# Moving small steps within a fused attention and expert kernel: where sums are finished, how token slots are made, when the hash codes come back, and how the first pair is laid out

## The chip, the cores and the metric

The kernel runs on one core of one Trainium2 chip. The metric is device time in microseconds (us). Engines are named as in the profile: PE multiplies matrices, PEld loads its weights, DVE, ACT and POOL work on vectors, and SP issues nearly all transfers from one queue, in order ("SPq"). L12 is line 12 of the kernel before.

## The reference

What is computed, cut to what matters here:

```python
q_bits = (einsum('bhsd,dk->bhsk', q, proj) > 0)      # 6 bits, k_bits alike
mask = q_bucket[:, :, :, None] == k_bucket[:, :, None, :]
scores = where(mask, q @ k.T / sqrt(D), -1e9)        # B 4, H 8, S 768, D 64
attn = exp(scores - max); attn /= attn.sum(-1) + 1e-09
x = (attn @ v) laid out as 3072 tokens of 512
probs = softmax(x @ w_gate)                          # 8 experts, the best one is taken
out[token] = gate * (relu(x[token] @ w1[e]) @ w2[e]) # w1 512 x 1024, w2 1024 x 512
```

## The kernel before

The attention works on 16 pairs of heads (`NPAIR` 4 per batch, `NPR` 16 in all). A pair has two groups of three blocks of 128 rows for two heads: twelve steps `(pr, g, jj, hh)`, 192 in all. The loop over `steps` is written with one step as its unit, and PE, DVE, ACT and SP run their instructions in just the order of the program; POOL's instructions are placed by a scheduler, apart from those wrapped in `in_turn`, which keep the program's order among themselves. Here `n` is the step in the group, and (g, n) names a place in a pair.

In step i the program issues the scores of step i + 2 (`scores`, L229 and L230 on PE, then the row maximum L232 and one or two small operations L233, L236 on DVE), the exponent of step i + 1 (`expo`, L248 on ACT, which also adds up the row into `sums`), the turning of the probabilities of step i or i - 1 (on PE and ACT, L273 and L276, or for half of the blocks through DRAM: four transfers `moved<-pd` L258, one back `pq<-moved` L261 two steps later, and a DVE transposition L264 six steps after the block), and in odd steps the product with V of the group before (`av`, L291). PSUM has two tiles for scores, so scores of step i + 2 wait for the exponent of step i.

Beside this stand slower threads:

- **Sums.** In step 5 of a group `av_evac` copies the product of the group before and adds 1e-9 to its sums: on POOL (L306, `in_turn`) in nearly all groups. Two steps later, `out_and_route` takes the reciprocal on DVE (L307), and `av_out` multiplies by it (L324).
- **Next pair's operands.** `PREPARE` lists at which place `q_operands`, `k_operands` (three POOL operations each, L160 to L162 and L169 to L171) and `pair_codes` (PE L146, DVE L148, POOL L149) are issued. The codes go to DRAM (`codes_out`, L175) and come back reshaped as rows of the second operand (`codes_back`, two transfers `c<-coded`, L180), which the scores L230 read.
- **Routing.** When a batch's four pairs are done, `route` makes pieces which run one to a step from the list `light`: `logits`, `gather_heads`, `one_hot`, `pause`, `ranks`, `rows`. Group 0's `rows` falls at (1, 3) of the second pair after, group 1's at (0, 4) of the next. In `rows` DVE makes the slots (L388 to L391) and POOL writes the rows to DRAM with three indirect transfers (L393). `gather_heads` and `av_out` use the same single PSUM tile `misc`, which `one_hot` reads last (L371).
- **The start.** `first_k` and `first_q` build the first pair's operands; `CLEARS` says in which steps the eight 910 KB fills of `xs` are issued.

After step 191 and a last routing, the experts follow: eight times two layers of matmuls on PE, with each operand split in two parts.

## Time and profile before

| | us |
|---|---|
| median of 3 runs | 755.05 |
| lowest and highest | 750.77 and 755.68 |
| the profiled execution's own time | 751.78 |
| its span, first to last instruction | 749.6 |
| first row maximum of step 0 / of step 12 / of step 192's last | 9.23 / 40.13 / 455.65 |

The span stretches from the first instruction to the last; the profiled execution's own time lies 2.2 us above it. A timeline row gives start, duration, engine, line, operation, tiles and, in brackets, how long its engine stood idle before it and what ended that. A row of a stretch (windows) gives its length, the busy time of each engine, the share of the full TensorE clock granted, and what the transfers took.

### The profile page before, as it was taken

The numbers are of one execution on the slowest core, as the hardware profiler recorded it, in microseconds if no ns is written. First come the engines' busy times: TensorE is split into PE (matmuls) and PEld (weight loads), VectorE is DVE, ScalarE is ACT, GpSimd is POOL, SyncE is SP. The second block draws the span as 40 slices with busy tenths as digits, with TensorE's granted clock in tenths as the row PEclk, the third lists the DMA queues.
The fourth block names the chain that finished last, engine by engine and source line by source line (L and its number), as shares of the span: only waits on it lengthen the run. The fifth ranks groups of instructions, "written<-read, shape, count | busy, mean of one in ns | idle before, by whom it ended". The sixth has DMA issues, their size and how long they took to land.

```text
span 749.6 us, 16080 instructions
## 1 busy us (share of the span) xinstructions
PE 706.7 (94%) x5735; PEld 621.4 (83%) x5735; DVE 520.1 (69%) x1028; ACT 465.3 (62%) x995; POOL 411.9 (55%) x401
## 2 busy tenths in 40 slices
PE   5999999988999979999979898999999999999996
PEld 2788887777887768887768787999999999999994
DVE  6668887867888867888868676674646464675741
ACT  5788987867988767898766674352434343443430
POOL 2775657485657575565675252105555647475471
PEclk9999999999999998999989999999999999999999
DMA  8969888877888877887885621646475565757521
GB/s 276 298 175 266 249 238 265 273 216 236 261 237 251 281 237 200 273 256 216 259 269 153 164 85 45 169 133 193 128 191 138 176 167 178 198 172 209 172 76 45
DMA packets 110081, 150.33 MB, mean 201 GB/s; under 512 B 12548, under 2 KB 77990, under 8 KB 109992
## 3 DMA queue, kind: packets, MB, share of 16 engines
q1 hardware_dynamic: 105016, 136.52, 63.6%
q0 software_dynamic: 4976, 12.69, 4.8%
q8 instruction: 47, 0.77, 0.4%
q14 instruction: 42, 0.34, 0.2%
HBM read 94.23 MB, written 55.18 MB: 199 GB/s over the span
## 4 chain that ended last, share of the span: by engine, by line
issue 20%; POOL 14%; PE 10%; DVE 4%; DMA 4%; SPq 1%; POOLq 0%; ACT 0%; another core or an unknown queue 0%; DVEq 0%
POOL y L1010 11%; PE o L291 3%; PE t L273 2%; PE s L229 2%; POOL yo L1008 2%; DMA y<-yo,tok 1%; PE s L230 1%; DVE m L232 1%; DMA xr<-xs 1%; DMA c<-coded 1%; PE s L722 1%; POOL tags L931 0%; DMA moved<-pd 0%; DVE pt L264 0%
## 5 line engine op out<-in xcount | busy, mean ns | idle before, releaser
L232 DVE TENSOR_REDUCE m<-s 128x1 f32<-128x768 f32 x192 | 182.8, 952 | 68.3 <-PE s L230 52.1
L229 PE MATMUL s<-k,q 128*128 128x512 f32 (+1 forms) x384 | 152.0, 396 | 19.7 <-ACT pd L248 11.8
L291 PE MATMUL o<-pt,vt 128*64 128x128 f32 x2304 | 148.6, 279 | 0.0
L291 PEld LDWEIGHTS o<-pt,vt 128*64 128x64 f32 x2304 | 125.6, 138 | 17.3 <-issue 11.5
L230 PE MATMUL s<-c 76*128 76x512 f32 (+1 forms) x384 | 127.0, 351 | 3.5 <-DMA c<-coded 3.4
L276 ACT COPY pt<-t 128x384 f32<-128x384 f32 x222 | 96.2, 485 | 54.3 <-PE t L273 51.5
L1010 POOL DMA_INDIRECT y<-yo,tags x88 | 104.1, 1183 | 24.9 <-issue 22.6
L229 PEld LDWEIGHTS s<-k,q 128*128 128x128 f32 x384 | 75.0, 195 | 51.3 <-POOL k L169 11.7
L248 ACT ACTIVATE p<-s,m 128x768 f32<-128x768 f32 x111 | 110.3, 994 | 10.7 <-DVE m L236 7.2
L273 PE MATMUL t<-ident,p 128*128 128x128 f32 x666 | 95.7, 281 | 0.0
L968 ACT ACTIVATE hh<-hps 128x352 fp32r<-128x352 f32 (+3 forms) x56 | 27.9, 500 | 97.5 <-PE hps L982 82.1
L230 PEld LDWEIGHTS s<-c 76*128 76x128 f32 x384 | 75.7, 197 | 14.2 <-issue 4.5
L273 PEld LDWEIGHTS t<-ident,p 128*128 128x128 f32 x666 | 77.9, 144 | 10.9 <-issue 9.8
L691 DVE TENSOR_TENSOR wlo<-wraw,whi 128x1024 fp32r<-128x1024 f32 x60 | 73.3, 1224 | 18.3 <-ACT whi L686 16.6
L248 ACT ACTIVATE pd<-s,m 128x768 f32<-128x768 f32 x81 | 80.3, 992 | 4.6 <-DVE m L236 0.7
L264 DVE STREAM_TRANSPOSE pt<-pq 128x768 f32<-128x768 f32 x81 | 78.5, 969 | 2.8 <-DMA pq<-moved 2.7
L1001 PE MATMUL hps<-hh,whi 128*128 128x448 f32 (+9 forms) x224 | 75.7, 338 | 0.0
L1001 PE MATMUL hps<-hl,whi 128*128 128x436 f32 (+6 forms) x224 | 75.6, 338 | 0.0
L1001 PE MATMUL hps<-hh,wlo 128*128 128x436 f32 (+6 forms) x224 | 75.6, 338 | 0.0
L982 PE MATMUL hps<-xh,whi 128*128 128x352 f32 (+3 forms) x224 | 75.2, 336 | 0.0
L982 PE MATMUL hps<-xl,whi 128*128 128x428 f32 (+6 forms) x224 | 74.9, 335 | 0.0
L982 PE MATMUL hps<-xh,wlo 128*128 128x428 f32 (+6 forms) x224 | 74.7, 334 | 0.0
(222 smaller groups left out, 1192.9 us busy)
## 6 DMA issues: line engine op xcount, KB each, us to landing
wraw<-w SPq DMA_DIRECT2D x64, 512.0 KB
moved<-pd SPq DMA_DIRECT2D x324, 96.0 KB
pq<-moved SPq DMA_DIRECT2D x81, 384.0 KB
qk<-qkd SPq DMA_DIRECT2D x30, 384.0 KB
xs<-zrow SPq DMA_DIRECT2D x8, 910.0 KB
vt<-v SPq DMA_DIRECT2D x16, 384.0 KB
coded<-cr SPq DMA_DIRECT2D x15, 192.0 KB
c<-coded SPq DMA_DIRECT2D x30, 72.0 KB
```

The costliest lines, as they stand in the source:

```text
L229: PE.matmul(out=s[:, c0:c1], lhsT=q1[:, qs], rhs=k1[:, c0:c1], start=True, stop=False)
L230: PE.matmul(out=s[:, c0:c1], lhsT=q2[0:KM, qs], rhs=k2[0:KM, c0:c1], start=False, stop=True)
L232: V.tensor_reduce(out=m[:, 0:1], in_=s[:, 0:S], axis=AX.X, op=ALU.max, negate=True)
L248: A.activation(to, of, AF.Exp, bias=m[:, 2:3], scale=m[:, 1:2], accum_out=sums[:, idx:idx + 1])
L264: V.transpose(out=pt()[:, hh].rearrange("p c (s j) -> p c s j", j=SQ), in_=q.rearrange("p s c i -> p c s i"))
L273: PE.transpose(out=t[:, i * P:i * P + P], in_=p[:, kc * P:kc * P + P], identity=ident)
L276: A.copy(out=dst, in_=src)
L291: PE.matmul(out=o[hh * D:hh * D + D, jj * P:jj * P + P], lhsT=vt[:, kc, hh * D:hh * D + D], rhs=pt[:, hh, kc], start=kc == 0, stop=kc == N ...
L691: loeng.tensor_tensor(out=lo[:, i:i + step], in0=cell["t"], in1=bf(hi[:, i:i + step]), op=ALU.subtract)
L982: PE.matmul(out=hps[:, 0:w], lhsT=wt[:, c, fs], rhs=xt[:, c, 0:w], start=n == 0, stop=n == 3 * NDC - 1)
L1001: PE.matmul(out=yps[:, 0:w], lhsT=wt[:, f, ds], rhs=ht[:, 0:w], start=n == 0, stop=n == 3 * NFC - 1)
L1010: rows_apart("out", G.indirect_dma_start(out=out_seg, out_offset=bass.IndirectOffsetOnAxis(ap=tags[:, i, 0:1].bitcast(I32), axis=0), in_=y ...
```

## The change

It has six parts. (1) The addition of 1e-9 to a group's sums is issued in step 0 of the next group, on POOL, in all groups but the last, and no longer in step 5. (2) `rows` takes the slot as a row maximum that is written as an integer (there is one non-zero entry) in place of a sum, and adds 1e-9 through a tensor operand `tiny` in place of a constant; the cast is gone, and the first of its three POOL transfers is held in the program's order. (3) Group 1's routing too has a `pause` behind `one_hot`, and group 0's `rows` issues the next piece, `av_out`, in the same step. (4) `codes_back` stands in step (1, 0) ahead of the returning `pq` transfer and the loads, and for the last pair in step (0, 5) of the pair before. (5) In the first pair `pair_codes` goes ahead of the second half of `first_q`, which is issued one step later; the scaling of the second head's codes comes behind the second exponent; two constant copies on DVE move to step 4; the next pair's operands and codes are prepared earlier. (6) `CLEARS` is earlier by a step or two.

```diff
-        if defer:
-            in_turn(G.tensor_scalar(out=sums, in0=sums, scalar1=1e-9, scalar2=None, op0=ALU.add))
             divide.append(lambda: V.reciprocal(out=inv, in_=sums.rearrange("p (j h) -> p j h", h=2)))
         else:
-            V.tensor_scalar(out=sums, in0=sums, scalar1=1e-9, scalar2=None, op0=ALU.add)
...
+        if n == 0 and prev is not None:
+            in_turn(G.tensor_scalar(out=prev[2], in0=prev[2], scalar1=1e-9, scalar2=None, op0=ALU.add))
...
         def rows():
-            V.tensor_scalar(out=mx[:, :, 1:2], in0=mx[:, :, 1:2], scalar1=1e-9, scalar2=None, op0=ALU.add)
-            V.reduce_sum(out=mx[:, :, 3:4], in_=pos, axis=AX.X)
+            V.reduce_max(out=slot, in_=pos, axis=AX.X)
+            V.tensor_tensor(out=mx[:, :, 1:2], in0=mx[:, :, 1:2], in1=tiny.unsqueeze(1).broadcast_to([P, 3, 1]), op=ALU.add)
             V.reciprocal(out=x[:, :, :, SEG + 1], in_=mx[:, :, 1:2].broadcast_to([P, 3, NG]))
-            V.tensor_copy(out=slot, in_=mx[:, :, 3:4])
...
+                if jj == 0 and b + 1 < B:
+                    in_turn(ins)
+            if not g and b + 1 < B:
+                light.pop(0)()
...
-        return [logits, gather_heads, one_hot, pause, ranks, rows] if not g and b + 1 < B else [logits, gather_heads, one_hot, ranks, rows]
+        return [logits, gather_heads, one_hot, pause, ranks, rows] if b + 1 < B else [logits, gather_heads, one_hot, ranks, rows]
...
-        {(0, 1): [(pair_codes, ())], (0, 3): [(q_operands, (0,)), (k_operands, (0,))], (0, 5): [(q_operands, (1,)), (k_operands, (1,)), (codes_out, ())],
-         (1, 1): [(codes_back, ())]},
+        {(0, 1): [(pair_codes, ())], (0, 2): [(q_operands, (0,)), (codes_out, ())], (0, 3): [(k_operands, (0,))], (0, 4): [(q_operands, (1,))],
+         (0, 5): [(k_operands, (1,)), (codes_back, ())]},
...
-         (0, 5): [(k_operands, (1,))], (1, 0): [(codes_back, ())]})
+         (0, 5): [(k_operands, (1,))]})
...
-    CLEARS = (2, 3, 3, 4, 6, 8, 10, 12)
+    CLEARS = (1, 1, 2, 3, 4, 6, 8, 10)
...
-        for queue in (later, returns):
-            while queue and queue[0][0] <= i:
-                queue.pop(0)[1]()
+        while later and later[0][0] <= i:
+            later.pop(0)[1]()
+        if (g, n) == (1, 0) and 0 < pr < NPR - 2 or (pr, g, n) == (NPR - 2, 0, 5):
+            codes_back(pr + 1)
+        while returns and returns[0][0] <= i:
+            returns.pop(0)[1]()
...
-        if 1 <= i < 3:
-            first_q(i - 1, 384)()
-        if i == 3:
+        if 2 <= i < 4:
+            first_q(i - 2, 384)()
+        if i == 4:
             start.close()
+            V.tensor_copy(out=tri, in_=lsb[:, 0:P])
+            V.tensor_copy(out=run, in_=eoff[:, 1])
         if i + 1 < len(steps):
             run_expo(i + 1)
+        if i == 0:
+            weigh()
```

In the third batch's routing, in pair 13, POOL's rows of the kernel before are these: the second head's q operands, the rows of group 1, the second head's k operands, and then the sums of (12, 1) and of (13, 0).

```order
L160 CAST q1_5390<-qk_5149 64x768
L161 TENSOR_TENSOR q1_5390<-qk_5149,q1_5390 64x768
L162 CAST c2_5278<-qk_5149 64x768
L393 DMA xs_60<-xr_3948,slot_5089 25600x520 x3
L169 CAST k1_5458<-qk_5149 64x768
L170 TENSOR_TENSOR c2_5278<-qk_5149,k1_5458 64x768
L171 CAST k1_5458<-qk_5149 64x768
L306 TENSOR_SCALAR sums_5008<-sums_5008 128x6
L306 TENSOR_SCALAR sums_5225<-sums_5225 128x6
```

In the changed kernel POOL has at the beginning of pair 13 (first row: group 0's sums of pair 12, then group 0's rows, then the sums of (12, 1)):

```order
L815 TENSOR_SCALAR sums_4795<-sums_4795 128x6
L395 DMA xs_60<-xr_3734,slot_4868 25600x520 x3
L815 TENSOR_SCALAR sums_5007<-sums_5007 128x6
L171 CAST k1_5275<-qk_5066 64x768
L172 TENSOR_TENSOR c2_5276<-qk_5066,k1_5275 64x768
```

The sums of (12, 1), `sums_5008` before and `sums_5007` now, have moved from behind the second head's k operands of pair 13 to ahead of its first head's, past thirteen POOL operations and the three transfers of group 1's rows.

SP's queue in pair 14, before: the codes of pair 15 go out, and come back behind the blocks moved next, a load of V, four loads of token rows and the first weights.

```order
L175 DMA coded1_62<-cr_5750 128x384
L261 DMA pq_5704<-moved3_66 128x768
L258 DMA moved0_63<-pd_5837 32x4x192 x4
L138 DMA vt_5873<-v 128x768
L618 TENSOR_LOAD best_i_165
L647 DMA xr0_5886<-xs_60 32x9x130
L682 DMA wraw_5896<-w1 128x1024
L180 DMA c2_5678<-coded1_62 12x4x384 x2
```

And now:

```order
L177 DMA coded1_62<-cr_5747 128x384
L266 DMA pq_5701<-moved3_66 128x768
L182 DMA c2_5675<-coded1_62 12x4x384 x2
L263 DMA moved0_63<-pd_5836 32x4x192 x4
L140 DMA vt_5871<-v 128x768
```

The two transfers that bring the codes back have moved ahead of all of these.

PE in steps 1 and 2 of the first pair, before: the hash bits of q's second half (L214), then those of the next pair (L146, four matmuls that share the tile `misc` with it), then turning.

```order
L230 MATMUL s_244<-c2_159 128x256
L214 MATMUL misc_253<-qr_133,pj_68 32x384
L146 MATMUL misc_261<-qk_146,pj_68 32x384
L146 MATMUL misc_261<-qk_148,pj_68 32x384
L273 MATMUL t_270<-ident_67,p_231 128x128 x3
L229 MATMUL s_281<-k1_161,q1_160 128x512
```

And now:

```order
L235 MATMUL s_246<-c2_159 128x256
L148 MATMUL misc_257<-qk_148,pj_68 32x384
L148 MATMUL misc_257<-qk_150,pj_68 32x384
L278 MATMUL t_266<-ident_67,p_229 128x128 x3
L234 MATMUL s_277<-k1_161,q1_160 128x512
```

L214 (now L219) no longer stands between the scores and the next pair's bits; it comes one step later.

## Rows read from the trace of the kernel before

**Rows 1.** Stretches of pairs 7, 5 and 6; length, PE, PEld, DVE, ACT, POOL busy, PEclk.

```profile
198.26:222.73 24.47, 24.38 (x245) 20.29 (x243) 20.40 (x35) 21.85 (x52) 15.32 (x15) 1.00 0.89 259
140.88:172.62 31.74, 25.75 (x258) 21.41 (x257) 24.59 (x54) 22.18 (x55) 23.50 (x24) 1.00 0.86 266
172.62:198.26 25.64, 25.64 (x245) 21.64 (x244) 20.35 (x35) 21.80 (x51) 13.49 (x15) 0.94 0.78 212
```

**Rows 2.** Waits over the whole span: us in total, times, longest us.

```profile
POOL cr L149 <- issue: 41.6, 10, 7.7
...
DVE inv L307 <- POOL sums L306: 10.8, 3, 3.7
...
PE misc L323 <- DVE lg L371: 2.9, 3, 1.0
...
DVE pt L264 <- DMA pq<-moved: 2.7, 3, 1.6
```

**Rows 3.** Timeline of pair 13, 379 to 389 us.

```profile
379.62 0.96 POOL L393 DMA_INDIRECT xs<-xr,slot  x1 [0.31 <-issue]
...
384.31 0.56 POOL L306 TENSOR_SCALAR sums<-sums 128x6 f32<-128x6 f32 x2
384.59 0.19 DVE L307 RECIPROCAL inv<-sums 128x6 f32<-128x6 f32 x1 [3.43 <-POOL sums L306]
...
388.89 0.77 PE L229 MATMUL s<-k,q 128*128 128x512 f32 x1 [3.80 <-ACT pd L248]
```

**Rows 4.** The stretches with PE's clock at half; columns as in rows 1.

```profile
18.92:22.33 3.41, 3.41 (x18) 2.26 (x10) 0.62 (x1) 1.36 (x3) 1.26 (x1) 0.50 1.06 318
172.52:175.93 3.41, 3.41 (x20) 2.99 (x20) 1.97 (x3) 2.49 (x7) 3.23 (x4) 0.50 0.88 242
278.33:285.16 6.83, 5.55 (x28) 4.97 (x30) 4.00 (x8) 4.74 (x12) 6.55 (x6) 0.50 0.85 275
387.56:394.39 6.83, 5.50 (x28) 4.92 (x30) 4.18 (x9) 4.40 (x10) 6.30 (x6) 0.50 0.87 279
421.69:425.10 3.41, 3.41 (x16) 3.22 (x15) 2.21 (x5) 1.94 (x4) 0.71 (x1) 0.50 0.18 70
```

**Rows 5.** Timeline of pair 14: SP's queue, and PE when the codes arrive.

```profile
403.86 0.34 SPq L175 DMA_DIRECT2D coded<-cr  x1
...
408.20 2.60 SPq L258 DMA_DIRECT2D moved<-pd  x4
...
414.61 0.81 SPq L180 DMA_DIRECT2D c<-coded  x2
...
421.30 0.47 PE L230 MATMUL s<-c 76*128 76x512 f32 x1 [3.09 <-DMA c<-coded]
```

**Rows 6.** Timeline of the first pair, 18 to 26 us.

```profile
18.65 1.30 PE L146 MATMUL misc<-qk,pj 128*32 128x384 f32 x8 [1.89 <-DVE c L222]
...
22.63 0.96 DVE L232 TENSOR_REDUCE m<-s 128x1 f32<-128x768 f32 x1 [2.02 <-PE s L230]
...
25.40 0.82 POOL L160 CAST q<-qk 64x768 fp32r<-64x768 f32 x1
```

**Rows 7.** L388 and L391 (min/median/max ns), and one timeline meeting.

```profile
L388 DVE TENSOR_SCALAR mx<-mx x7: 151/160/1391, 139.6 to 460.4; 128x3 f32<-128x3 f32 x7
...
L391 DVE CAST slot<-mx x7: 104/106/1733, 139.9 to 460.7; 128x3 int32<-128x3 f32 x7
...
374.10 1.83 POOL L161 TENSOR_TENSOR q<-qk,q 64x768 fp32r<-64x768 f32 x1
...
374.22 1.73 DVE L391 CAST slot<-mx 128x3 int32<-128x3 f32 x1
```

**Rows 8.** A DVE operation with two SBUF inputs beside a POOL one; its group's mean.

```profile
L691 DVE TENSOR_TENSOR wlo<-wraw,whi 128x1024 fp32r<-128x1024 f32 x60 | 73.3, 1224 | 18.3 <-ACT whi L686 16.6
...
664.13 0.86 POOL L1008 TENSOR_TENSOR yo<-yt,tags 128x384 f32<-128x384 f32 x1
...
664.44 1.65 DVE L691 TENSOR_TENSOR wlo<-wraw,whi 128x1024 fp32r<-128x1024 f32 x1 [0.41 <-ACT whi L686]
```

More of the change, by code (lines that the diff above doesn't have):

```diff
@@ L83, in lsh_attention_moe_kernel @@
     V.memset(ones, 1.0)
+    tiny = const.tile([P, 1], F32, name="tiny")
+    V.memset(tiny, 1e-9)
     run = const.tile([P, E], F32, name="run")
@@ L201, in put_codes, with weigh_codes @@
             for x in range(2):
+                r0 = D + 32 * x
+                V.tensor_scalar(out=k2[D:KM, 384 * x:384 * x + 384], in0=cpss[x], scalar1=0.0, scalar2=cols[r0:r0 + NCODE, 2:3], op0=ALU.is_gt, op1=ALU.subtract)
+        def weigh_codes():
+            for x in range(2):
                 cs = slice(384 * x, 384 * x + 384)
-                r0 = D + 32 * x
-                V.tensor_scalar(out=k2[D:KM, cs], in0=cpss[x], scalar1=0.0, scalar2=cols[r0:r0 + NCODE, 2:3], op0=ALU.is_gt, op1=ALU.subtract)
                 A.activation(k2[D:KM, cs], bf(k2[D:KM, cs]), AF.Copy, bias=0.0, scale=BIG)
-        return put_codes
+        return put_codes, weigh_codes
     def first_q(hh, c0):
@@ L387, in rows @@
             x = xrows[(b, g)]
-            V.tensor_scalar(out=mx[:, :, 1:2], in0=mx[:, :, 1:2], scalar1=1e-9, scalar2=None, op0=ALU.add)
-            V.reduce_sum(out=mx[:, :, 3:4], in_=pos, axis=AX.X)
+            V.reduce_max(out=slot, in_=pos, axis=AX.X)
+            V.tensor_tensor(out=mx[:, :, 1:2], in0=mx[:, :, 1:2], in1=tiny.unsqueeze(1).broadcast_to([P, 3, 1]), op=ALU.add)
             V.reciprocal(out=x[:, :, :, SEG + 1], in_=mx[:, :, 1:2].broadcast_to([P, 3, NG]))
-            V.tensor_copy(out=slot, in_=mx[:, :, 3:4])
             for jj in range(3):
-                rows_apart("xs", G.indirect_dma_start(out=xs, out_offset=bass.IndirectOffsetOnAxis(ap=slot[:, jj, :], axis=0),
-                                                      in_=x[:, jj].rearrange("p g w -> p (g w)"), in_offset=None))
+                ins = G.indirect_dma_start(out=xs, out_offset=bass.IndirectOffsetOnAxis(ap=slot[:, jj, :], axis=0),
+                                           in_=x[:, jj].rearrange("p g w -> p (g w)"), in_offset=None)
+                rows_apart("xs", ins)
+                if jj == 0 and b + 1 < B:
+                    in_turn(ins)
+            if not g and b + 1 < B:
+                light.pop(0)()
         def pause():
             pass
-        return [logits, gather_heads, one_hot, pause, ranks, rows] if not g and b + 1 < B else [logits, gather_heads, one_hot, ranks, rows]
+        return [logits, gather_heads, one_hot, pause, ranks, rows] if b + 1 < B else [logits, gather_heads, one_hot, ranks, rows]
     def last_route(sums, o):
@@ L538, in lsh_attention_moe_kernel @@
     SY.dma_start(out=lsb[:, 0:P], in_=tri_in)
-    V.tensor_copy(out=tri, in_=lsb[:, 0:P])
     SY.dma_start(out=eoff, in_=eoff_in)
-    V.tensor_copy(out=run, in_=eoff[:, 1])
     SY.dma_start(out=ids, in_=ids_in)
@@ L748, in lsh_attention_moe_kernel @@
     in_order.enter_context(tc.manual_schedule(engines={PE.engine, V.engine, A.engine, SY.engine}))
-    first_codes = [first_k(0, V), first_q(0, 0)]
-    for f in first_codes:
+    put, weigh = first_k(0, V)
+    put_q = first_q(0, 0)
+    for f in (put, weigh, put_q):
         f()
@@ L753, in lsh_attention_moe_kernel @@
     run_scores(1)
-    first_codes = [first_k(1, G), first_q(1, 0)]
+    put, weigh = first_k(1, G)
+    put_q = first_q(1, 0)
     run_expo(0)
-    for f in first_codes:
-        f()
+    put()
+    put_q()
     SY.dma_start(out=h0[0][:, 384:S], in_=q2d[0][:, 384:S])
-    CLEARS = (2, 3, 3, 4, 6, 8, 10, 12)
+    CLEARS = (1, 1, 2, 3, 4, 6, 8, 10)
     prev, due, extra = None, [], {}
```

## The prediction

> **What bounds the kernel now.** I read the stretches of single pairs first. In an undisturbed pair (pair 7) PE is busy 24.38 of 24.47 us [rows 1]: the attention is bound by PE, and what can be won there is PE's idle time and the time at the lower clock. Pair 5, in which a batch is routed, lasts 31.74 us with PE busy 25.75, so PE stands still for 6.0; pair 6 behind it is all busy and still takes 25.64, at a granted clock of 0.94 [rows 1]. The reader sees that the loss comes in the pairs with routing, which return three times.
>
> Next I read the waits. The longest that DVE has on POOL is the reciprocal of the sums: 10.8 us in three waits [rows 2]. The timeline of the third shows the order: POOL issues the rows' indirect transfers until 380.6, then three operand operations, and only then the sums, at 384.31; DVE has waited 3.43 us for them, and PE, whose next scores need an exponent that needs DVE's row maximum, restarts at 388.89 after 3.80 [rows 3]. Then I read the granted clock: after each of these waits it is at half, with PE busy 3.41, 5.55 and 5.50 us at 1.2 GHz; likewise after the wait for the codes of pair 15 and in the first pair [rows 4].
>
> **The change part by part.**
>
> *A, the sums.* The addition needs only the last exponent of its group, and is now issued before the next pair's operands. At the place of the reciprocal it has been done for about a pair, as it stood behind thirteen operations and three transfers and now stands ahead of them. All three waits go: 10.8 us [rows 2]. At double clock the slow work would have taken half: (3.41 + 5.55 + 5.50) / 2 = 7.2 [rows 4]. Together 18.0. What is late next at this place is the DVE transposition, which needs its block back from DRAM, and POOL itself, still as late as before with the k operands; those are wanted only in the next pair. I take off 2 for such remainders: **16**, between 9 (waits gone by half, the clock not) and 18. One POOL instruction per pair is new at the head of the k operands and waits there for the last exponent; behind it POOL holds all of the next pair's operands. The cover is POOL's own idle time ahead of the codes, 41.6 us in ten pairs, 4.2 each [rows 2]; I cost it at 0, and if the cover were gone it would be about 1 us a pair, that is 14.
>
> *B, the last codes.* They were issued at 414.61, behind loads, and PE got them at 421.30 after 3.09 idle [rows 5]; the 3.41 us at half clock behind it cost 1.7 [rows 4]. The codes went out at 403.86, and SP's next transfer but one was at 408.20, so the codes can now be issued by then, 6.4 us earlier or more. The wait was 3.1, so the codes are there in time. The first weights are then next in the queue; they are issued about a microsecond earlier too. 3.1 + 1.7 = 4.8, I take **4.5**, between 2 and 4.8.
>
> *C, the first pair.* PE waited 1.89 us for DVE to release `misc` [rows 6], and 3.41 us ran at half clock, 1.7 [rows 4]; the reordering takes both away: 3.6, and up to 1.1 more from the turning behind it. But POOL now has the next pair's q operands of head 0 (0.82 + 1.83 + 0.82 = 3.5 us by [rows 6, 7]) ahead of the subtraction for head 1's second half, which step 7's scores need, one step later than it was. That gives part of it back as a new PE wait. Ends: 4.7 and, if all 3.5 shows and the clock falls once more (1.7), 3.6 - 5.2 = -1.6. I take the middle, **2.0**.
>
> *D, the gap behind `one_hot`.* PE's transposition waited 2.9 us in three times for DVE to have done with `misc` [rows 2]; with a step between, this goes. In exchange `gather_heads` of group 1 falls in an even step, where DVE also transposes a moved block, and `av_out` shares a step with `rows`. DVE is busy 24.59 of 31.74 there [rows 1], not full, but two score tiles give little slack. Ends 2.9 and -2.9; I take **1.0**, nearer to the row that is named than to a cost that no row names.
>
> *E, `rows`.* The constant addition took 160 ns at the median and up to 1391, the cast 106 and up to 1733; the cast that began at 374.22 ended at 375.95, when POOL's operation of 374.10 ended at 375.93 [rows 7]. DVE was held until POOL was through. One such meeting falls in each of the three pairs: at most 3 x 1.63 = 4.9 us of DVE. The change replaces both, so the ends are 4.9 and 0. What replaces the addition reads two tensors in SBUF; the nearest row with that form was held too, 1.65 against a mean of 1.22 beside a POOL operation [rows 8]. So I take less than half: **2**.
>
> The Trainium skill speaks against this part: its page SBUF — State Buffer, section "Who interferes with whom", says that casts and operations with a scalar can take the port pair that DVE shares with POOL, that a reduction never does, and that an operation with two SBUF inputs contends with a POOL operation that reads SBUF, the later one being blocked until the first ends. By that rule the maximum is free but the new addition is held like the old one. The trace agrees for the cast [rows 7] and, by 0.4 us, for the two inputs [rows 8]. By the rule the term would be near 0.5, without it near 4.9.
>
> *The rest.* The codes of 13 pairs go ahead of the returning block on SP; the two issues took 0.81 us [rows 5]. The block is transposed four steps later, some 8 us in a pair of 24.47 [rows 1]; that hides it, and the whole of DVE's waiting for such blocks is 2.7 us in three times [rows 2]. I cost it at 0, and at 13 x 0.8 = 11 if nothing covers it. The fills of `xs` and the copies on DVE move within the first steps; they lie beside the same PE work: 0. The experts, behind the last routing, keep their order and only begin earlier.
>
> Sum: 16 + 4.5 + 2 + 1 + 2 = 25.5. Against the profiled execution's own 751.78 this gives 726.3. The runs' median lies 3.3 above that execution, its lowest 1.0 below; of this I add 1.7: **728**.
>
> **The rivals.**
>
> *1. The new addition is held as the old one was.* POOL's q operands fall just there, at the same place as before; for it speaks the held two-input row [rows 8], against it that DVE now reaches `rows` with the integer maximum first, which may shift the meeting. E is then 0.5 instead of 2: 728 + 1.5 = 729.5. This is the result of the Trainium skill's rule on the shared port, named above. Chance 0.22.
>
> *2. The stall moves.* DVE, freed from the sums, soon stands before the next block from DRAM or before the transfers that the busy queue (a share of 0.86 in pair 5 [rows 1]) delivers late; PE still waits once per batch, and the clock still falls. Then A gives half of 18, that is 9, B 4.5, and C, D and E together nothing: 13.5, which is 740. For it speaks that DVE has waited for such blocks before [rows 2]; against it that the next blocks at that place had been issued long before. Chance 0.15.
>
> *3. The sums still wait.* If POOL were late at the head of the pair too, the reciprocal would find the sums late as before, and only B would be won: 755.05 - 4.5 = 750.5. Against it speaks the order: what stands ahead of the sums there ends before the pair's first exponents. Chance 0.03.
>
> *4. Slower: the codes push the blocks.* In each of 13 pairs the two code transfers stand ahead of the returning block. If that block lands last, DVE's transposition comes 0.8 us late [rows 5], PE idles, and its clock drops as it did after the waits above, 1.7 each [rows 4]: 13 x 2.5 = 32.5 against 25.5 won, so 755.05 - 25.5 + 32.5 = 762. It decides from the point where the block is less than 0.8 us early; three waits of up to 1.6 show that this happens [rows 2], but only three times in the whole attention. Chance 0.04.
>
> **How the numbers follow.** My forecast has 0.56, the rivals 0.22, 0.15, 0.03 and 0.04. The range reaches down to 719, where A is 18, B 4.8, C 4.7, D 2.9 and E 4.9 (35.3 off 755.05 is 719.8), and up to 741, which takes in rival 2. A measurement of this kernel can tell about 1% from no change, 7.5 us. Faster by more than that are the forecast and rivals 1 and 2, 0.93, of which I give 0.01 to no change, as rival 2 may come out smaller: 0.92; within 1% then 0.04; slower 0.04.
>
> **What would show it right or wrong.** Right: no wait of the reciprocal on POOL's sums; pairs 5, 9 and 13 near 26 us, pairs 6 and 10 near 24.5 at full clock; no PE wait on `c<-coded` behind pair 14; PE's clock at half only at the very start and around the last routing. In the first pair, the row maximum of step 4 before 20 us instead of at 22.63 [rows 6], and a wait of step 7's scores on POOL. In `rows`, no operation above 0.3 us would speak for E, an addition near 1.4 for rival 1. Wrong: the reciprocal waits gone but pairs 5, 9 and 13 still above 29 us (rival 2), or ordinary pairs longer than 24.5 with waits on `pq<-moved` (rival 4).

## The result and the profile after

The changed kernel takes 731.88 us, median of 4 runs (727.23 to 740.92), beside 752.91 (749.56 to 755.68) for the kernel before on the same chip; the ratio is 0.9702 [0.9627, 0.9777]. Run once more beside the experiments it took 732.38 (728.97 to 735.4) against 749.52: 0.9754 [0.9682, 0.9826]. That is 17 to 21 us won, where 25.5 were forecast. The execution that was profiled first (740.92) is a slow run, with 10.24 us at half clock in the first pair and 3.41 in the experts, which the change doesn't touch: medians here are of all runs, ratios of the fast ones alone, and the profile read below is that of the second measurement (728.97, span 726.8).

First the waits of the changed kernel up to 440 us (us in total, times, longest), the end of the attention; rows of PE, then of DVE.

```profile
PE s L234 <- ACT p L253: 2.9, 9, 0.5
PE s L234 <- POOL q L226: 1.9, 1, 1.9
PE s L235 <- DMA c<-coded: 1.2, 2, 1.0
...
DVE m L237 <- PE s L235: 33.5, 78, 1.9
DVE pt L269 <- DMA pq<-moved: 13.9, 10, 3.3
```

The reciprocal's 10.8 us on POOL's sums [rows 2] have no row any more, nor has the release of `misc` by the routing. The wait of 3.09 us for the codes of pair 15 [rows 5] is gone; 0.98 of the 1.2 that is left is at pair 6. In their place DVE's transposition now waits 13.9 us in ten times for its block from DRAM, where it waited 2.7 in three [rows 2].

Next pair 5 by stretches, after (columns as in rows 1, then DMA share and GB/s): up to step 9, the middle of the second group, and the last 7.5 us.

```profile
138.73:152.43 13.70, 13.43 (x140) 11.09 (x139) 12.30 (x33) 11.00 (x27) 10.51 (x11) 1.00 0.87 282
152.43:159.89 7.46, 7.46 (x79) 6.45 (x77) 6.06 (x14) 7.11 (x17) 6.42 (x7) 1.00 0.62 164
159.89:167.39 7.50, 5.76 (x48) 4.89 (x47) 3.92 (x7) 4.68 (x12) 4.00 (x6) 0.90 0.99 320
```

PE is busy 20.89 of the first 21.16 us; what PE still loses in the pair it loses in the last 7.5 us, 1.74 us of idle time and some of the clock (0.90), and there the DMA engines are full (0.99), after a stretch in which they were at 0.62. The timelines of DVE and PE show what ends the waits there:

```profile
163.00 0.15 DVE L238 TENSOR_SCALAR m<-m 128x1 f32<-128x1 f32 x1
166.48 0.98 DVE L269 STREAM_TRANSPOSE pt<-pq 128x768 f32<-128x768 f32 x1 [3.33 <-DMA pq<-moved]
...
163.62 0.47 PE L234 MATMUL s<-k,q 128*128 128x512 f32 x1 [0.76 <-POOL k L173]
165.07 0.47 PE L235 MATMUL s<-c 76*128 76x512 f32 x1 [0.98 <-DMA c<-coded]
```

The two engines do not wait for the same thing. PE's 1.74 us are 0.76 for POOL's k operands, which stand behind the row step's transfers on POOL, and 0.98 for the codes. DVE's 3.33 us for the block delay the next row maximum, and with it the pair length used below; PE shows no idle time behind them here, but it runs at half clock just then. PE at the end of pair 9 (two rows) and of pair 13:

```profile
268.11 0.47 PE L234 MATMUL s<-k,q 128*128 128x512 f32 x1 [0.87 <-issue]
269.61 0.47 PE L235 MATMUL s<-c 76*128 76x512 f32 x1 [1.03 <-POOL sums L815]
...
375.95 1.52 PE L296 MATMUL o<-pt,vt 128*64 128x128 f32 x22 [0.44 <-DVE pt L269]
```

Only the last, 0.44 us, is put down to the block.

The stretches of the attention at half clock, five before [rows 4], are two:

```profile
25.93:29.34 3.41, 3.26 (x14) 2.67 (x13) 3.31 (x8) 1.86 (x5) 3.28 (x3) 0.50 0.75 224
165.87:169.28 3.41, 3.41 (x22) 2.99 (x22) 2.76 (x4) 1.63 (x4) 1.59 (x2) 0.50 1.04 384
```

### The profile page after: what moved, and what is told of

Its sections match the earlier page's. It is cut to its first block, busy times and chain, and to the rows that moved or that the text cites. A ratio compares the mean times of both kernels' runs of the same rounds, so it can differ in the third digit from the quotient of the medians.

```text
span 738.7 us, 16077 instructions
## 1 busy us (share of the span) xinstructions
PE 706.2 (96%) x5735; PEld 620.3 (84%) x5735; DVE 518.1 (70%) x1020; ACT 463.3 (63%) x995; POOL 407.5 (55%) x403
## 4 chain that ended last, share of the span: by engine, by line
issue 21%; POOL 13%; PE 10%; DMA 4%; DVE 3%; ACT 1%; SPq 1%; POOLq 0%; another core or an unknown queue 0%; ACTq 0%; DVEq 0%
POOL y L1026 11%; PE o L296 3%; PE s L234 2%; PE t L278 2%; POOL yo L1024 2%; DMA y<-yo,tok 1%; PE s L235 1%; DVE m L237 1%; DMA pq<-moved 1%; DMA xr<-xs 1%; PE s L727 1%; ACT p L253 1%; DMA y<-yo,tags 0%; ACT pd L253 0%; DMA xs<-xr,slot 0%
## 5 line engine op out<-in xcount | busy, mean ns | idle before, releaser
L237 DVE TENSOR_REDUCE m<-s 128x1 f32<-128x768 f32 x192 | 182.5, 951 | 54.3 <-PE s L235 36.4
L296 PEld LDWEIGHTS o<-pt,vt 128*64 128x64 f32 x2304 | 125.4, 138 | 19.3 <-issue 10.8
L253 ACT ACTIVATE p<-s,m 128x768 f32<-128x768 f32 x111 | 110.3, 993 | 12.3 <-DVE m L241 8.8
L1026 POOL DMA_INDIRECT y<-yo,tags x88 | 101.4, 1152 | 24.9 <-issue 22.6
L278 PE MATMUL t<-ident,p 128*128 128x128 f32 x666 | 94.1, 278 | 0.0
L984 ACT ACTIVATE hh<-hps 128x352 fp32r<-128x352 f32 (+3 forms) x56 | 27.8, 499 | 103.6 <-PE hps L998 91.6
L235 PEld LDWEIGHTS s<-c 76*128 76x128 f32 x384 | 75.1, 195 | 10.8 <-issue 1.3
L1024 POOL TENSOR_TENSOR yo<-yt,tags 128x512 f32<-128x512 f32 (+3 forms) x25 | 23.2, 949 | 93.7 <-DVE yt L1019 93.6
```

What stands on the lines that cost most here:

```text
L235: PE.matmul(out=s[:, c0:c1], lhsT=q2[0:KM, qs], rhs=k2[0:KM, c0:c1], start=False, stop=True)
L237: V.tensor_reduce(out=m[:, 0:1], in_=s[:, 0:S], axis=AX.X, op=ALU.max, negate=True)
L253: A.activation(to, of, AF.Exp, bias=m[:, 2:3], scale=m[:, 1:2], accum_out=sums[:, idx:idx + 1])
L278: PE.transpose(out=t[:, i * P:i * P + P], in_=p[:, kc * P:kc * P + P], identity=ident)
L296: PE.matmul(out=o[hh * D:hh * D + D, jj * P:jj * P + P], lhsT=vt[:, kc, hh * D:hh * D + D], rhs=pt[:, hh, kc], start=kc == 0, stop=kc == N ...
L1026: rows_apart("out", G.indirect_dma_start(out=out_seg, out_offset=bass.IndirectOffsetOnAxis(ap=tags[:, i, 0:1].bitcast(I32), axis=0), in_=y ...
```

## The experiments

In the table the last two columns add up pair lengths, from the first row maximum (L237; L232 before) of a pair to that of the next, in the profile of each kernel: pairs 5, 9 and 13, in which a batch is routed, and pairs 6, 10 and 14 behind them. Times are medians; ratios are to the kernel before in the same session. The runs of the last but one spread from 728.49 to 743.08 and give no interval. Each pair length is read from one execution. The program of these six pairs is the same in the changed kernel's two profiles, with the old first pair and with the later q operands, and there the first of the two columns comes to 85.46 to 87.98 and the second to 74.37 to 74.75: a difference of 2.5 us or less in the first says nothing. A late row maximum lengthens one pair and shortens the next, so the two columns are best added.

| kernel | us | ratio, 95% | 5, 9, 13 | 6, 10, 14 |
|---|---|---|---|---|
| before | 747.5 to 752.9 | 1 | 96.51 | 83.36 |
| changed, second profile | 732.38 | 0.9754 [0.9682, 0.9826] | 86.72 | 74.45 |
| without the sums' move | 745.29 | 0.9896 [0.9823, 0.9968] | 94.20 | 79.31 |
| the sums' move alone | 741.87 | 0.9896 [0.9815, 0.9977] | 86.93 | 78.20 |
| old first pair | 728.93 | 0.9697 [0.9616, 0.9779] | 87.87 | 74.37 |
| middle codes late again | 740.25 | 0.9878 [0.9798, 0.9957] | 90.60 | 79.86 |
| old routing order | 730.95 | 0.9745 [0.9693, 0.9797] | 87.41 | 74.40 |
| old row step | 730.94 | 0.9751 [0.9692, 0.9810] | 85.46 | 74.77 |
| q operands a step later in pair 0 | 728.87 | 0.9747 [0.9689, 0.9804] | 85.46 | 74.75 |
| early loads | 730.38 | 0.9765 [0.9732, 0.9797] | 89.53 | 75.66 |
| both of these | 729.38 | 0.9763 [0.9733, 0.9794] | 87.55 | 75.43 |
| early loads, middle codes late | 739.70 | none | 92.23 | 80.26 |
| one block less through DRAM | 727.16 | 0.9696 [0.9639, 0.9753] | 80.76 | 76.27 |

**The changed kernel again.**

> The changed kernel once more. Theory 1 (its profiled execution, 740.92, carried about 10 us at half clock in the first pair and some more in the experts that most executions do not have): the profile now ends between 725 and 733, with no half-clock stretch above 3.5 us in the first 40 us. Rival (the half clock in the first pair belongs to the new order of the start): the first pair again ends its 12 steps at about 42 us with the clock at half behind the wait for POOL's subtraction L226, whatever the total.

Theory 1 holds: 728.97 us, one stretch of 3.41 us at half clock in the first pair, and step 12's row maximum at 38.95 us, where the first profile had 42.05. The longer stretch comes back in other executions (see the old first pair below).

**Without the sums' move**: the addition stands again at the end of its group, all else as changed.

```diff
-        if n == 0 and prev is not None:
-            in_turn(G.tensor_scalar(out=prev[2], in0=prev[2], scalar1=1e-9, scalar2=None, op0=ALU.add))
...
         if defer:
+            in_turn(G.tensor_scalar(out=sums, in0=sums, scalar1=1e-9, scalar2=None, op0=ALU.add))
```

> The changed kernel with the addition to the sums back in step 5. Theory 1 (the sums are the largest term): the reciprocal waits for POOL's sums again, 3 times 2.5 to 3.7 us, with the clock at half behind them, and the time rises by 8 to 16 over the changed kernel. Rival (the wait for the block from DRAM, 13.0 us in the changed kernel's profile, has taken the place of the sums): the reciprocal waits, the DRAM wait shrinks by as much, and the time rises by less than 5.

**The sums' move alone**: the kernel before with the same edit forward.

> The kernel before with the earlier addition to the sums alone. Theory 1: 8 to 16 below the kernel before, the wait on c<-coded behind pair 14 still 3 us. Rival (a wait for the block from DRAM takes its place): less than 5 below, and waits on pq<-moved of 2 to 4 us at the end of pairs 5, 9 and 13.

Waits of DVE up to 460 us without the move, then with the move alone:

```profile
DVE inv L312 <- POOL sums L311: 13.3, 3, 5.6
...
DVE pt L269 <- DMA pq<-moved: 2.3, 5, 1.1
```

```profile
DVE pt L264 <- DMA pq<-moved: 3.1, 5, 1.2
```

The move takes the wait away by itself. It is worth 12.9 us by the medians (745.29 - 732.38) and 12.3 by the six pairs when all else is there, and 14.7 by the six pairs when it is alone. By the medians it is then worth only 7.7, by the interval 2 to 14; the profile without the move is of an execution of 750.14 us, that with the move alone of one of 736.45, so the pairs may flatter it. Alone, it leaves DVE a wait of 3.1 us for blocks, not 13.9: what makes DVE wait at the block is what the other parts add to it. The rival of the first test was right in this half: without the move the wait for the block shrinks by 11.6 us.

**Old first pair**: order of the turnings, operands, codes and `CLEARS` of the first pair as before.

```diff
-        if 2 <= i < 4:
-            first_q(i - 2, 384)()
+        if 1 <= i < 3:
+            first_q(i - 1, 384)()
...
-        {(0, 1): [(pair_codes, ())], (0, 2): [(q_operands, (0,)), (codes_out, ())], (0, 3): [(k_operands, (0,))], (0, 4): [(q_operands, (1,))],
-         (0, 5): [(k_operands, (1,)), (codes_back, ())]},
+        {(0, 1): [(pair_codes, ())], (0, 3): [(q_operands, (0,)), (k_operands, (0,))], (0, 5): [(q_operands, (1,)), (k_operands, (1,)), (codes_out, ())],
+         (1, 1): [(codes_back, ())]},
```

> The changed kernel with the first pair laid out as before (order of codes and second halves, scaling, copies, fills). Theory 1 (the new start loses what it gains, since head 1's second half waits on POOL behind the next pair's operands): step 12's row maximum at about 40 us instead of 42, and the time 0 to 3 below the changed kernel. Rival (the prediction's term, a gain of 2 in most executions): the time 1 to 4 above the changed kernel.

From its first row maximum to that of the second pair the first pair takes 30.90 us before, 30.55 here, and 29.69 in the changed kernel; the time is no longer for the old order, rather 3.4 us shorter, which the intervals allow to be chance. In the other profiles with the new order it takes 29.72 to 30.03, but 31.01 to 32.78 in four in which the clock stood at half for 6.83 or 10.24 us there (10.24 in the changed kernel's first profile, from 26.91 on): 1.2 won at the best, 1.9 lost at the worst. The old order varies too: with the sums' move alone the first pair, laid out as before, takes 31.78 with 6.83 us at half clock. PE's timeline of the changed kernel (first fence) and of the version with the q operands a step later (second) shows what became of the wait:

```profile
25.05 0.50 PE L234 MATMUL s<-k,q 128*128 128x512 f32 x1 [1.87 <-POOL q L226]
```

```profile
24.54 0.50 PE L234 MATMUL s<-k,q 128*128 128x512 f32 x1 [0.25 <-ACT p L253]
28.12 0.75 PE L234 MATMUL s<-k,q 128*128 128x512 f32 x1 [1.94 <-ACT p L253]
```

**Middle codes late again**: in all but the last pair they come back at the end of step (1, 0).

```diff
-        if (g, n) == (1, 0) and 0 < pr < NPR - 2 or (pr, g, n) == (NPR - 2, 0, 5):
+        if (pr, g, n) == (NPR - 2, 0, 5):
             codes_back(pr + 1)
...
+        if not last and (g, n) == (1, 0) and 0 < pr < NPR - 2:
+            codes_back(pr + 1)
```

> The changed kernel, but the middle pairs' codes come back at the end of step (1,0) again, behind the loads and the returning block; the codes of the last pair stay early. Theory: DVE waits for the returning block (13.9 us in 10 in the second profile of the changed kernel, against 2.7 before) because two code transfers stand ahead of it. Then the wait on the block falls to about 3 us, pairs 5, 9 and 13 shorten from 28.7 to 29.2 us to about 27.5, and the kernel is 3 to 5 us faster than the changed one. Rival: DVE, freed from the sums, merely comes earlier to a block whose transfer takes some 6.5 us anyway. Then the wait stays above 10 us, these pairs stay at 28.5 to 29.5, and the time is within 2 us of the changed kernel's.

The theory falls, and the rival's number too: the wait for blocks stays (12.1 us in 10), but the kernel loses 9.3 us in the six pairs. In pairs 5, 9 and 13 the block's read is issued 1.7, 2.1 and 0.7 us earlier than in the changed kernel, and its transposition still begins within 0.3 us of the same place. PE now waits for the codes themselves; its total, and the first of the waits, at pair 6:

```profile
PE s L235 <- DMA c<-coded: 10.2, 4, 3.8
...
167.87 0.47 PE L235 MATMUL s<-c 76*128 76x512 f32 x1 [3.36 <-DMA c<-coded]
...
160.74 1.80 SPq L182 DMA_DIRECT2D c<-coded  x2
```

The codes issued at 160.74 are there 7.1 us later. In the changed kernel those issued at 159.85 are there by 165.07, 5.2 later.

```profile
159.85 1.92 SPq L182 DMA_DIRECT2D c<-coded  x2
```

In pairs 5, 6, 9, 10 and 13 this version differs from the one with the sums' move alone by the routing order and the row step only, and those five pairs take 142.6 us against 135.4: with the codes late these two parts lose 7.3 us. In the changed kernel, with the codes early, the five take 134.9 (134.0 to 136.1 in the four profiles of its program).

**Old routing order**: no empty step behind group 1's `one_hot`, `av_out` not taken forward.

```diff
-            if not g and b + 1 < B:
-                light.pop(0)()
...
-        return [logits, gather_heads, one_hot, pause, ranks, rows] if b + 1 < B else [logits, gather_heads, one_hot, ranks, rows]
+        return [logits, gather_heads, one_hot, pause, ranks, rows] if not g and b + 1 < B else [logits, gather_heads, one_hot, ranks, rows]
```

> The changed kernel with the old order of routing in the second group: no empty step behind the one-hot, and the output tile of the group of before not taken forward. Theory (as predicted): the gap is worth 1.0 us, and DVE's hold on misc, 2.9 us in three before, comes back: slower by about 1 us, with pairs 5, 9 and 13 about 0.3 us longer. Rival: as pairs 5, 9 and 13 end with a wait for the returning block, what the gap wins is given back there: these pairs stay within 0.2 us and the time is the same, or shorter where the end of routing comes a step earlier and lets the block be issued earlier (pairs 5, 9 and 13 at 28 us or less).

**Old row step**: the constant addition, the sum and the cast instead of the maximum and `tiny`.

```diff
-            V.reduce_max(out=slot, in_=pos, axis=AX.X)
-            V.tensor_tensor(out=mx[:, :, 1:2], in0=mx[:, :, 1:2], in1=tiny.unsqueeze(1).broadcast_to([P, 3, 1]), op=ALU.add)
+            V.tensor_scalar(out=mx[:, :, 1:2], in0=mx[:, :, 1:2], scalar1=1e-9, scalar2=None, op0=ALU.add)
+            V.reduce_sum(out=mx[:, :, 3:4], in_=pos, axis=AX.X)
...
+            V.tensor_copy(out=slot, in_=mx[:, :, 3:4])
```

> The changed kernel with the old row step: addition of a constant, sum, cast. Theory (as predicted): the casts and the scalar addition are held again while POOL works, 1 to 1.7 us once or twice in pairs 5, 9 and 13, 2 us together, and these pairs grow by 0.5 to 0.7 us each. Rival: what is held in the row step lies ahead of a wait for the returning block, and the block is no later for it; the rows show the held operations, up to 1.7 us, but the pairs keep 28.7 to 29.2 us and the time is the same within 1 us.

In both, the waits come back as expected, and no loss of time can be told. PE with the old routing:

```profile
PE misc L326 <- DVE lg L374: 2.9, 3, 1.0
```

The row step's operations (duration in ns: shortest, median, longest), old in the first fence (addition L391, cast L394), new in the second (maximum L391, addition L392):

```profile
L391 DVE TENSOR_SCALAR mx<-mx x7: 150/160/1689, 137.1 to 439.5; 128x3 f32<-128x3 f32 x7
...
L394 DVE CAST slot<-mx x7: 104/105/1742, 137.4 to 439.8; 128x3 int32<-128x3 f32 x7
```

```profile
L391 DVE TENSOR_REDUCE slot<-pos x7: 156/166/169, 137.0 to 439.2; 128x3 int32<-128x24 f32 x7
...
L392 DVE TENSOR_TENSOR mx<-mx,tiny x7: 153/155/570, 137.1 to 439.3; 128x3 f32<-128x3 f32 x7
```

These are the longest of seven in one profile each, and the addition's varies: see rival 1 below.

So the gains of both parts are there and go nowhere. The starts of the row maxima in pair 5 show it; its length up to step 9, and of its last three steps:

| kernel | up to step 9 | last three | pair 5 |
|---|---|---|---|
| before | 21.57 | 10.17 | 31.74 |
| the sums' move alone | 21.54 | 7.36 | 28.90 |
| old routing order | 21.33 | 8.00 | 29.32 |
| old row step | 20.57 | 7.70 | 28.28 |
| changed | 18.64 | 10.01 | 28.66 |
| middle codes late again | 18.90 | 10.90 | 29.81 |
| early loads | 18.67 | 11.26 | 29.93 |
| one block less through DRAM | 20.01 | 6.51 | 26.53 |

With gap and new row step together the second group runs 2.9 us earlier than with the sums' move alone, and the last three steps take 2.65 longer: something fixed in time stands at the end of the pair. DVE's rows for the block there, with the old routing order and with the old row step (the pairs begin at 140.14 and 138.80):

```profile
168.55 0.98 DVE L269 STREAM_TRANSPOSE pt<-pq 128x768 f32<-128x768 f32 x1 [1.81 <-DMA pq<-moved]
```

```profile
166.18 0.98 DVE L269 STREAM_TRANSPOSE pt<-pq 128x768 f32<-128x768 f32 x1 [1.52 <-DMA pq<-moved]
```

DVE gets there 26.6 and 25.9 us into the pair, in the changed kernel 24.4; the block comes at 28.4, 27.4 and 27.8. One thing the table doesn't show: pairs 4, 8 and 12 take 26.48 to 26.49 with the old routing order and 26.87 to 27.11 in the changed kernel, and no profile of either order lies outside 26.43 to 26.49 and 26.79 to 27.56. There the new order loses about 0.4 us each.

**The q operands a step later** in the first pair:

```diff
-        {(0, 1): [(pair_codes, ())], (0, 2): [(q_operands, (0,)), (codes_out, ())], (0, 3): [(k_operands, (0,))], (0, 4): [(q_operands, (1,))],
+        {(0, 1): [(pair_codes, ())], (0, 2): [(codes_out, ())], (0, 3): [(q_operands, (0,)), (k_operands, (0,))], (0, 4): [(q_operands, (1,))],
```

> The changed kernel, but the q operands of head 0 of the second pair are made one step later, so that the subtraction for the second half of head 1 goes first on POOL. Theory: the wait of 1.9 us of step 7's scores on POOL, and the half clock that follows it (3.4 to 10.2 us at half), come from these operands: the wait goes, the row maximum of step 12 falls from 39 to 42 us to about 37, and the kernel is 2 to 4 us faster. Rival: PE waits for something else a step later (DVE's misc, or the second pair's operands, now later), step 12 stays at 39 us or later, and nothing is won.

The wait on POOL goes, and from its first row maximum on step 6 is reached in 13.51 us instead of 15.56; but PE then waits 1.94 us at 28.12, for an exponent (second fence above), the clock falls there, and the first pair takes 29.77 against 29.69. The rival holds for the time; step 12's row maximum comes at 38.18 us, between the theory's 37 and the rival's 39.

**Early loads**: in pairs 5, 9 and 13 the two loads of heads go out at (0, 3) and (0, 5).

```diff
-        if (g, n) in ((1, 1), (1, 3)) and pr + 2 < NPR:
+        if (g, n) in (((0, 3), (0, 5)) if pr % NPAIR == 1 and pr > NPAIR else ((1, 1), (1, 3))) and pr + 2 < NPR:
```

> The changed kernel, but in pairs 5, 9 and 13 the two loads of the heads of the pair after next go out at steps (0,3) and (0,5) instead of (1,1) and (1,3): the same bytes, earlier. Theory: the ends of these pairs are bound by transfers. In the second profile of the changed kernel the DMA engines are 0.56 and 0.63 busy in the middle of pairs 9 and 5 (256.3 to 264.0, 152.5 to 160.0), and 0.97 and 0.99 in the last 7.5 us of them, where the returning blocks and the two loads meet. With the loads in the slack the last step falls from 5.1 to 5.4 us to about 2.5 to 3, pairs 5, 9 and 13 to 26 to 27.5, and the kernel is 4 to 7 us faster. Rival: the blocks are late because they leave DRAM one after another behind one another's writes, whatever else is moved: the last step stays above 4.5, the pairs at 28.5 to 29.2, the time within 1.5 us.

The same with the q operands a step later, and the same with the middle codes late:

> The early loads, and with them the q operands of the second pair a step later in the first pair. Theory: both gains add, 1 to 3 us of the first pair to 4 to 7 of the loads: 5 to 10 us faster than the changed kernel. Rival: the first pair's later operands give back at its end what its step 7 wins, and the time is that of the early loads alone within 1 us.

> The early loads, but the middle pairs' codes behind the returning block again, as in the kernel before. Theory: the codes came 2.7 to 3.8 us late at pairs 6, 10 and 14 (which made the kernel some 9 us slower than the changed one) as their transfers ran among blocks and loads in the busiest stretch; with the loads taken out of it the codes land in time or less than 1 us late, and the kernel stands within 3 us of the one with early loads. Rival: it is the issue behind the returning block that makes the codes late, whatever the traffic: they come over 2 us late in three places again, and the kernel is 6 to 10 us slower than with early loads alone.

The three theories miss; the rivals of the last two hold by the medians, though the runs with late codes spread too far to settle it, and their pairs are from an execution of 743.08 us. The last 7.5 us of pair 5 with early loads:

```profile
161.17:168.67 7.50, 3.68 (x35) 3.00 (x34) 3.66 (x6) 2.77 (x7) 5.61 (x6) 0.92 1.02 308
```

They are as full as without (1.02), PE is busy in less than half of them, the six pairs take 165.2 against 161.2, and the wait for blocks grows to 17.9 us in 12. PE waits for the codes, 5.3 us in three times, though they are early in the program; with the codes late, 7.3 in two. SP's queue with early loads shows why this does not clear the loads:

```profile
149.13 0.44 SPq L135 DMA_DIRECT2D qk<-qkd  x1
...
157.50 0.44 SPq L135 DMA_DIRECT2D qk<-qkd  x1
...
160.48 2.31 SPq L182 DMA_DIRECT2D c<-coded  x2
```

The second load now goes out beside the row step's transfers and ahead of the block and the codes in the same queue: it was moved from one part of the busy stretch to another, and 84 of POOL's packets now fall behind 163 us, where 3 did. Loads issued later were not tried.

What else the block and the codes meet is seen in the changed kernel's transfers, by queue (packets, MB, share of 16 engines), between 159 and 163 us:

```profile
q0 software_dynamic: 237, 0.79, 52.2%
q1 hardware_dynamic: 704, 0.62, 46.3%
```

q0 holds the three indirect transfers of the row step, which POOL issues from 156.37 on; q1 is SP's queue with everything else. Blocks, codes and loads share less than half of the engines for 4 us. From 163 to 167.39 us POOL's queue is done and SP's own fills them; there the block's read runs beside the first load, of the same 384 KB:

```profile
q1 hardware_dynamic: 917, 1.34, 101.5%
q0 software_dynamic: 3, 0.00, 0.3%
```

```profile
161.87 0.34 SPq L266 DMA_DIRECT2D pq<-moved  x1
162.25 0.48 SPq L135 DMA_DIRECT2D qk<-qkd  x1
```

**One block less through DRAM**: on top of the later q operands, the block of step (0, 4) of pairs 5, 9 and 13 is turned by PE.

```diff
-    MOVES = {(pr, g): (0, 2, 4) for pr in range(1, NPR - 2) for g in range(2)} | {(14, 0): (0, 2), (14, 1): (0,)}
+    MOVES = {(pr, g): (0, 2, 4) for pr in range(1, NPR - 2) for g in range(2)} | {(pr, 0): (0, 2) for pr in (5, 9, 13)} | {(14, 0): (0, 2), (14, 1): (0,)}
```

> The version with the second pair's q operands a step later in the first pair, and with one block less through DRAM in each of pairs 5, 9 and 13: the block of step (0,4), which is written just ahead of the row step's three transfers and read back among them, is turned by PE instead (6 PE transpositions of 0.8 us together and 2 ACT copies more, 0.79 MB of traffic less, no DVE transposition at step (1,4)). Theory: DVE's wait at the last step of these pairs is for this block, which the row step's transfers (192 packets of 4160 bytes, a share of 0.4 to 0.7 of the DMA engines in 159 to 163 us of the second profile) hold up together with the codes. Without it the waits for blocks fall from 14.0 us to under 7, the last step from 3.3 to 5.7 us to 2.4 to 3, the pairs to 26 to 27.5, and the kernel is 2 to 5 us faster than the version it is built on (728.87). Rival: the codes or the next block, written in the same stretch, come as late: the pairs stay at 27.6 to 29.7 and the time within 1.5 us, or longer by the 0.8 us of PE work in each.

The wait and the pairs come as the theory says. DVE's wait up to 440 us, and the two later stretches of pair 5:

```profile
DVE pt L269 <- DMA pq<-moved: 4.9, 7, 1.3
```

```profile
152.36:157.69 5.33, 4.92 (x49) 4.16 (x47) 3.75 (x9) 4.84 (x13) 4.90 (x5) 1.00 0.52 149
157.69:165.19 7.50, 7.50 (x76) 6.48 (x77) 5.51 (x11) 6.42 (x15) 6.10 (x7) 1.00 0.94 273
```

PE has no idle time in the last 7.5 us, the clock stays full, and the three pairs last 80.76 us against 85.46 in the version it is built on; the pairs behind them give back 1.5 of that (76.27 against 74.75). It has the lowest time of all (723.26) and the lowest median, 727.16, but its runs reach up to 737.14 and its interval overlaps that of the changed kernel; that it beats the kernel before is shown, that it beats the changed one is shown in the pairs and in the wait, not in the time: the theory wanted 2 to 5 us less than 728.87, and the medians of the two sessions differ by 1.7. The block that stays is the one DVE waited for, and its transposition on DVE goes with it. So the run shows what this block's way through DRAM costs, not that any other traffic taken out of the stretch would do as well.

## Why the prediction was right, and where it was off

*Right in the mechanism.* The addition's move takes away the reciprocal's wait, with nothing else needed. Pairs 6 and 10 came to 24.14 and 24.07 us; no wait of pair 15 on its codes is left; the row maximum of step 4 in the first pair comes at 17.56 us, and step 7's scores wait for POOL, 1.87 us, as put. Two signs were missed: PE's clock still falls once at the end of pair 5 (165.87), and pairs 5, 9 and 13 stay above 26. By the gain the forecast was further off than by the time: 25.5 against 21.0, and against 17.1 in the second measurement, which lies nearer to rival 2's 13.5. That 728 lies so near to 731.88 is in part the luck of the runs.

*A, the sums, forecast 16.* Measured 12.3 to 14.7 by the pairs, inside its bounds of 9 to 18; by the medians 12.9, or 7.7 when it is alone. The remainder was sized 2 and named right, "the DVE transposition, which needs its block back from DRAM", and POOL, "still as late as before with the k operands"; with the whole change it is more, a last step of 5.38 us in pair 5 and one more stretch at half clock. Pairs 5, 9 and 13 came to 28.66, 28.84 and 29.22, well above the forecast's 26 and, in one of three, above the 29 from which rival 2 was to hold: the stall had moved, as rival 2 says, but only in part.

*B, the last codes, forecast 4.5.* Pair 14 takes 29.78 us with the sums' move alone and 26.24 in the changed kernel: 3.5. Without the sums' move it falls from 31.64 to 27.17: 4.5.

*C, D and E, forecast 2 + 1 + 2.* Each is worth nothing that these runs can tell. This is the step that failed. C's two ends were there, the 1.89 us gone and 1.87 us new on POOL; the middle between them was taken (1.55 by the ends given, not 2.0; for the 1.1 us "from the turning behind it" no row is named), and the first pair came out between 1.2 us shorter and 1.9 longer. D and E were priced as waits and held operations at DVE, and these come back when they are undone: 2.9 us on `misc`, up to 1.7 us in one cast. But they lie ahead of a block, codes and k operands that come when the transfers and POOL let them: DVE reached the block 2.2 us earlier than with the old routing order, and the block came 0.7 earlier. The forecast counted the gains on the path to the end, though it had read that the DMA engines are 0.86 busy in pair 5. Over the five pairs 5, 6, 9, 10 and 13 the changed kernel takes 134.9 us and the sums' move alone 135.4, and pairs 4, 8 and 12 are some 0.4 us longer each for D.

*The rest, costed at 0.* The middle codes' place was judged by the 0.8 us that it costs the block (in pair 5 the two issues took 1.92), and put at 0 or a loss. It is the other way: with D and E in place PE wants the codes earlier, and codes left behind the block would have cost 9.3 us in six pairs. It is the condition under which D and E cost nothing. That by itself it wins nothing is argued, not run: in the kernel before, the codes were late for pair 15 by 3.1 us and otherwise by 0.3 in all. Rival 4, which made of it 32.5 us of loss, had nothing to it: pair 7 takes 24.11 us.

So the sum comes to 12 to 15, 3.5 and nothing: 16 to 18, beside the 17 to 21 measured. Of the forecast's 25.5, the 5 of C, D and E were not there; the rest of the gap is A and B, each a little over-sized.

*Rival 1.* In the profile read above the new addition takes 570 ns at the longest, in the changed kernel's first 368. That was luck. Of eleven profiles with the new row step, seven have an addition of 1.24 to 1.76 us, as long as the old one's 1.69, while the integer maximum never takes more than 0.17. In the version with the q operands a step later, at pair 9:

```profile
258.01 1.81 POOL L163 TENSOR_TENSOR q<-qk,q 64x768 fp32r<-64x768 f32 x1
...
258.09 1.76 DVE L392 TENSOR_TENSOR mx<-mx,tiny 128x3 f32<-128x3 f32 x1
```

DVE's addition ends with POOL's operation, as the cast did in [rows 7]. So rival 1 is right in its mechanism: the new addition can be held as the old one was. Added up over pairs 5, 9 and 13, the time above each operation's median is 4.8 to 6.2 us in the three profiles with the old form and 0.3 to 3.6 with the new (4.8 in the kernel before, near the bound of 4.9, though in pairs 5 and 9 as two shorter holds); what E takes away for sure is the hold of the cast. With the old routing order the addition takes 1.64 us in pair 5 and in the changed kernel 0.15, so up to 1.5 of the 2.7 us between their step 9 is this and not the routing. The Trainium skill says (SBUF — State Buffer, "Who interferes with whom") that a reduction never contends with POOL and that an operation with two SBUF inputs contends with a POOL operation that reads SBUF. The runs agree for both. For the time no difference can be told.

*What held the block.* That the 0.79 MB of the row step's packets took 52.2% of the engines for 4 us, and that keeping this block out of DRAM ends the wait, is measured. That these packets delay the block is argued, since the row step's transfers themselves were not moved; and they can't be all of it, as they are through by 163 us and the block comes at 166.48, beside a load. How much is the row step's and how much the load's stays open, and so does what each of PE's three waits there, for codes, k operands and block, would cost by itself. The Trainium skill states (DMA: Bandwidth & Descriptors, "Issuing engines are not separate DMA queues") that transfers end on the same 16 DMA engines and interleave, whichever engine began them. The rows by queue agree: between 159 and 163 us the two queues take 52.2% and 46.3%.

## What to carry to other kernels

A wait that is removed is worth what lies between it and the next thing that is fixed in time: look for the transfer at the end of the stretch, and price all edits ahead of it together, not one by one. A part that measures as worthless can be the condition for another, so undo parts from the whole and try them alone. Where transfers bound only a few microseconds, it helped to keep the late block out of them, and the same loads a little earlier did not help; look first where a moved transfer lands, since one of those loads ran in the busy stretch all the same. And read a held operation in more than one profile: whether two engines meet can change from one execution to the next.

## What the runs showed beyond this

A share near 1 of the DMA engines says little of where the bytes come from: with two loads of 384 KB issued before the last 7.5 us of pair 5 that stretch was as full, as part of the row step's packets moved into it. And between 152.43 and 159.89 us the engines stood at 0.62 with 164 GB/s, just ahead of the stretch at 0.99 with 320, so the average of 0.86 over such a pair hid both.
